# Masking the first batch's scores with one more TensorE product of constants per head

## Chip, cores and metric

One core of a Trainium2 chip runs the whole program. The metric is the device time of one execution in microseconds (us): the kernel before took 805.56 us, the median of three runs between 805.19 and 806.23.

## What is computed

Three stages on an input of 4 batches, 8 heads, 576 positions and 64 channels per head; the stages' results feed one another.

```python
scores = scale * np.matmul(q, k.transpose(0, 1, 3, 2))
mask = block_i >= block_j            # blocks of 64 positions
scores = np.where(mask, scores, -1000000000.0)
attn = softmax(scores); x = attn @ v # then heads side by side: (4, 576, 512)
k = np.maximum(xk @ w_k, 0.0); v = k * k @ w_v     # xk, xr: x mixed with its shifted self
x = sigmoid(xr @ w_r) * v
h = np.maximum(xt @ w_tok1, 0.0) @ w_tok2; u = x + h.T
out = u + np.maximum(u @ w_ch1, 0.0) @ w_ch2
```

The mask works in blocks of 64 positions. Where 128 rows of queries are taken at a time, the last 64 columns are masked for the upper 64 rows alone: a corner of 64 by 64.

## The kernel before

Attention goes by batch, by half of the queries (`hf` 0: positions 0 to 255, `hf` 1: the other 320) and by pair of heads (four pairs). Inside a half, `unit` (L515) works on 128 query rows, `j` = 0, 1 in the first half and 2, 3, 4 in the second; `j` = 4 has only 64 rows and takes both heads in one. A unit is a chain: `scores` (TensorE, into one of two PSUM tiles `s`), `mask` (VectorE memset of the corner to -8e9, L538, units j below 4 only), `largest` (VectorE maximum, L544), `bias` (L551 or L553), `exps` (ScalarE, L563), `sums` and `inverse` (L571 to L581), `first` (ScalarE, fp16 part of the probabilities, L587), `second` (VectorE, the rest in fp16, L593), `turn` (DMA transpose issued by SyncE, L599). `pv` (L602) multiplies the transposed probabilities by v (L646) and `total` brings them to SBUF as `xt` (L655, L657).

Behind attention, `channel_mix` (products at L751 and L756, into two PSUM tiles `l`) needs the four `xt` of a half: `mix` makes from them `mt` (L720, L726), `xh` (L732) and `xl` (L736). Then follow `front` (L914 to L966) and `back` (products at L764), which use TensorE almost alone.

Scores of batches 1 to 3 are made of three products of fp32r parts. Batch 0's are made of one product of plain fp32 operands (`load_qk` takes its short way for `b == 0`; `qk` at L504 then has one term). While batch 0's attention runs, the weights w_r, w_k and w_v are loaded and cut in high and low parts (`load_split`, `split_chunk`, L345 to L364), on ScalarE, VectorE and GpSimd.

The order on every engine is written out by a planner (`Plan.schedule`): each step has a cost, a due key, and reads and writes; for each engine the ready step with the smallest key is taken. Tables in `PLAN` (`lead_of`, `shift`, `lead_begin`) move the keys of a kind or a group of steps. Each engine then runs its list strictly in that order, waiting on semaphores.

```python
def mask():
    nc.vector.memset(s[:D, :, n - D:n], -8.0e9)
if j < 4:
    step("V", 0.14, ks, mask, r=[ts], w=[ts])
```

Of the kernel before, what the change touches and what calls it, by code (L numbers as in the profile page):

```python
# [8 lines left out]
F32 = mybir.dt.float32  # L9
# [41 lines left out]
        "attention.edge": -710.03, "back.<lambda>": 34.98, "back.g_group": -21.39, "back.g_high": -674.45,  # L51
        "back.g_low": -16.35, "back.rest": 162.8, "back.split": -271.85, "back.store": -779.77, "back.y_group":
        -49.32, "back.y_out": 128.07, "channel_mix.k_group": 0.52, "channel_mix.k_high": 122.36, "channel_mix.k_low":
        49.5, "channel_mix.k_out": 700.87, "channel_mix.r_group": -1.88, "channel_mix.r_out": 38.93,
        "channel_mix.square": -490.37, "channel_mix.store": 972.64, "channel_mix.v_group": -4.31, "channel_mix.v_out":
        138.59, "front.back_in": 734.14, "front.h1_high": -268.59, "front.h1_low": -80.29, "front.hidden": 281.6,
        "front.high": 274.43, "front.load": 776.08, "front.low": 678.84, "front.sum_u": 443.53, "front.turn": -120.46,
        "load_qk.high": 253.03, "load_qk.load": 185.56, "load_qk.low": 404.0, "load_qk.whole": 421.84,
        "load_v.gather": -15.3, "load_v.largest": -10.87, "load_v.load": 459.86, "load_v.one": 31.7, "load_v.power":
        182.97, "load_v.scale": 265.33, "load_v.spread": 478.19, "load_v.two": 729.5, "mix.here": -3.03, "mix.high":  # L60
        -14.49, "mix.low": 3.37, "mix.shifted": 147.07, "pv.products": -2.92, "pv.total": 92.69, "split_chunk.high":
        -63.89, "split_chunk.join": 6.76, "split_chunk.load": 143.85, "split_chunk.low": 282.21, "split_chunk.top":
        -112.45, "unit.bias": 105.96, "unit.exps": -239.76, "unit.first": -135.83, "unit.inverse": 471.77,
        "unit.largest": 1.71, "unit.mask": -0.69, "unit.scores": 481.59, "unit.second": 298.83, "unit.sums": 7.56,
        "unit.turn": -61.72,
# [15 lines left out]
        "attention.edge": 435.9, "back.<lambda>": 51.92, "back.g_group": -175.33, "back.g_high": -96.6, "back.g_low":  # L81
        174.47, "back.rest": 361.48, "back.split": 9.57, "back.store": -676.96, "back.y_group": -435.13, "back.y_out":
        -318.97, "channel_mix.k_group": -3.92, "channel_mix.k_high": 34.48, "channel_mix.k_low": 295.9,
        "channel_mix.k_out": 61.25, "channel_mix.r_group": -2.48, "channel_mix.r_out": 355.16, "channel_mix.square":
        181.93, "channel_mix.store": 254.58, "channel_mix.v_group": -1.74, "channel_mix.v_out": -95.22,
        "front.back_in": -799.64, "front.h1_high": -94.53, "front.h1_low": 327.36, "front.hidden": 242.72,
        "front.high": 556.49, "front.load": 51.98, "front.low": -83.46, "front.sum_u": 165.73, "front.turn": -324.84,
        "load_qk.high": -199.96, "load_qk.load": -251.86, "load_qk.low": 447.4, "load_qk.whole": 59.5,
        "load_v.gather": 96.8, "load_v.largest": -4.29, "load_v.load": 9.75, "load_v.one": 200.21, "load_v.power":
        74.15, "load_v.scale": -126.43, "load_v.spread": 91.47, "load_v.two": -460.37, "mix.here": 1.97, "mix.high":  # L90
        19.35, "mix.low": 63.96, "mix.shifted": 223.54, "pv.products": -1.86, "pv.total": 4.3, "split_chunk.high":
        191.37, "split_chunk.join": -2.04, "split_chunk.load": -58.89, "split_chunk.low": -104.87, "split_chunk.top":
        225.28, "unit.bias": 146.72, "unit.exps": 56.02, "unit.first": 220.91, "unit.inverse": -61.06, "unit.largest":
        0.1, "unit.mask": 86.57, "unit.scores": 187.42, "unit.second": -42.99, "unit.sums": -11.55, "unit.turn":
        -135.86,
# [14 lines left out]
def c_pe(n, k):  # L110
    return n / 2260 + 0.008 * k
# [194 lines left out]
class Kern:  # L306
# [71 lines left out]
    def attn_setup(self, pool):  # L378
        nc = self.nc
        self.eye = pool.tile([P, P], BF16, name="eye", bufs=1)  # L380
        self.ones = pool.tile([P, P], BF16, name="ones", bufs=1)
        self.step("G", 0.6, -1e3, make_identity, nc, self.eye, w=["eye"])
        self.step("V", 0.1, -1e3, nc.vector.memset, self.ones, 1.0, w=["ones"])
        self.pin = []
        for i in range(BUFS["pin"]):
            t = pool.tile([P, 2 * NJ * P], F16, name=f"pin{i}", bufs=1)
            self.step("V", 0.7, -1e3, nc.vector.memset, t, 0.0, w=[("pins", i)])
            self.pin.append(t)
# [115 lines left out]
    def qk(self, st, q0, parts):  # L504

        a, z = st["qk"][0], st["qk"][-1]
        terms = [a] if a is z else [a, (z[0], a[1]), (a[0], z[1])]
        for n, (q, k) in enumerate(terms):
            for o, e, k0, k1 in parts:
                self.nc.tensor.matmul(o, q[e, q0:q0 + P], k[e, k0:k1], start=n == 0, stop=n == len(terms) - 1)  # L510

    def unit(self, key, st, heads, j, begin):
# [857 lines left out]
```

## Time and profile before

| | us |
|---|---|
| median of three runs | 805.56 (805.19 to 806.23) |
| the profiled execution | 811.06 |
| its span, first to last instruction | 809.3 |
| TensorE busy in it | 763.7 (94%), granted clock 0.993 on average |
| VectorE busy | 477.3 (59%) |
| ScalarE busy | 419.2 (52%) |
| GpSimd busy | 181.3 (22%) |

The profile reports one execution. Its shares are means over stages of different kind, so it is read here by stretches: busy time of each engine in a stretch, the granted TensorE clock (1.00 is 2.4 GHz, 0.50 is 1.2 GHz), and the instructions in order of time with the idle time ahead of them in brackets. An instruction's duration on VectorE or ScalarE reaches a little into the next one's, so durations add up to somewhat more than the time taken.

### The profile page before, as it was taken

The page shows a single profiled execution, that of the slowest core. Times are in us where ns is not written, and L with a number is a line of the kernel's source. Part 1 is how long each engine was busy: PE and PEld are TensorE (multiplying, and loading weights), DVE is VectorE, ACT ScalarE, POOL GpSimd, SP SyncE. Part 2 cuts the span into 40 slices and gives each one's busy share as a digit, 9 for nine tenths or more (in the row PEclk, how much of TensorE's full clock was granted, in tenths as well). Part 3 has the DMA queues.
Part 4 walks back from the last instruction along what each step waited for, and adds up shares of the span by engine and source line. Part 5 has one row for each costly group of instructions (what it writes and reads, how often), then busy time and mean ns, then how long its engine had stood idle before and what let it go on. Part 6 is the DMA issues. An engine that isn't in the chain of part 4 may idle for free.

```text
span 809.3 us, 16129 instructions
## 1 busy us (share of the span) xinstructions
PE 763.7 (94%) x6120; PEld 661.7 (82%) x6120; DVE 477.3 (59%) x1194; ACT 419.2 (52%) x1070; POOL 181.3 (22%) x209
## 2 busy tenths in 40 slices
PE   2459999998999999999999999999999999999998
PEld 1227899887989999999999989998888888888886
DVE  7897898997798987789555687612212302301210
ACT  6887978687678795778564565502201201301100
POOL 3433524334145142432443222200000000000000
PEclk9999999999899999999999999999999999999999
DMA  8976964686465843566552654200000010000001
GB/s 272 269 189 106 201 148 115 146 170 120 113 138 125 159 117 93 117 140 113 191 180 84 232 170 141 78 27 1 14 26 1 14 39 14 1 26 14 14 13 40
DMA packets 136750, 84.30 MB, mean 104 GB/s; under 512 B 110944, under 2 KB 118240, under 8 KB 136160
## 3 DMA queue, kind: packets, MB, share of 16 engines
q1 hardware_dynamic: 136672, 83.27, 41.8%
q8 instruction: 48, 0.79, 0.4%
q14 instruction: 30, 0.25, 0.1%
HBM read 47.58 MB, written 9.44 MB: 70 GB/s over the span
## 4 chain that ended last, share of the span: by engine, by line
PE 81%; DVE 7%; DMA 5%; ACT 5%; issue 2%; SPq 0%; POOL 0%; ACTq 0%; DVEq 0%
PE b L764 37%; PE l L751 18%; PE l L756 9%; PE s L510 5%; PE o L646 4%; PE b L938 3%; PE b L959 3%; DMA pt<-pin 3%; DVE pin L593 2%; DMA wst<-in_w_k 1%; PE b L914 1%; DVE nm L544 1%; ACT pin L587 1%; ACT p L563 1%; DMA qkl<-in_w_v 1%
## 5 line engine op out<-in xcount | busy, mean ns | idle before, releaser
L1030 ACT ACTIVATE wy<-b 128x512 fp32r<-128x512 f32 (+1 forms) x60 | 33.3, 555 | 211.8 <-PE b L764 211.2
L764 PE MATMUL b<-uh,wx 128*128 128x512 f32 (+1 forms) x480 | 139.6, 373 | 0.0
L751 PE MATMUL l<-xh,wx 128*128 128x256 f32 (+1 forms) x768 | 123.7, 302 | 2.2 <-ACT r L792 1.8
L751 PEld LDWEIGHTS l<-xh,wx 128*128 128x128 f32 x768 | 107.9, 190 | 7.4 <-ACT r L792 2.0
L764 PE MATMUL b<-wy,c2a 128*128 128x512 f32 (+1 forms) x460 | 110.8, 367 | 0.0
L764 PEld LDWEIGHTS b<-uh,wx 128*128 128x128 f32 x480 | 87.2, 188 | 17.3 <-issue 0.2
L764 PEld LDWEIGHTS b<-wy,c2a 128*128 128x128 f32 x460 | 79.2, 189 | 15.3
L593 DVE SCALAR_TENSOR_TENSOR pin<-p,rs,pin 128x128 f16<-128x128 f32 (+4 forms) x112 | 77.0, 707 | 7.5 <-ACT pin L587 7.3
L1045 DVE TENSOR_TENSOR x<-b,x 128x256 f32<-128x256 f32 (+7 forms) x32 | 13.5, 454 | 114.8 <-PE b L764 114.8
L751 PE MATMUL l<-kh,wy 128*128 128x256 f32 (+1 forms) x512 | 78.1, 304 | 0.2 <-DVE ve L428 0.2
L646 PEld LDWEIGHTS <-vb 128*64 128x64 f16 x1920 | 52.9, 115 | 29.8 <-issue 13.7
L646 PE MATMUL o<-pt,vb 128*64 128x128 f16 (+1 forms) x1920 | 62.4, 220 | 14.3 <-DMA pt<-pin 7.2
L764 PE MATMUL b<-gx,wx 128*128 128x512 f32 x192 | 75.4, 393 | 0.0
L751 PEld LDWEIGHTS l<-kh,wy 128*128 128x128 f32 x512 | 71.5, 194 | 2.5 <-issue 1.4
L563 ACT ACTIVATE p<-s,nb 128x384 f32<-128x384 f32 (+4 forms) x112 | 61.6, 553 | 19.2 <-DVE nb L553 9.7
L587 ACT ACTIVATE pin<-p,rs 128x128 f16<-128x128 f32 (+4 forms) x112 | 63.2, 588 | 13.2 <-DMA pt<-pin 6.9
L756 PE MATMUL l<-xl,wx 128*128 128x320 f32 (+1 forms) x384 | 68.2, 300 | 0.0
L544 DVE TENSOR_REDUCE nm<-s 128x2 f32<-128x256 f32 (+4 forms) x80 | 63.6, 798 | 1.9 <-PE s L510 1.3
L756 PEld LDWEIGHTS l<-xl,wx 128*128 128x128 f32 x384 | 56.6, 190 | 2.1 <-issue 1.2
L1033 DVE SCALAR_TENSOR_TENSOR wy<-b,wy 128x512 fp32r<-128x512 f32 (+1 forms) x28 | 16.1, 576 | 62.8 <-ACT wy L1030 62.7
L1033 DVE SCALAR_TENSOR_TENSOR gx<-b,wy 128x512 fp32r<-128x512 f32 x32 | 21.9, 690 | 47.8 <-ACT wy L1030 47.8
L736 POOL TENSOR_TENSOR xl<-mt,xh 128x256 fp32r<-128x256 f32 (+1 forms) x32 | 28.4, 891 | 91.7 <-DVE xh L732 52.5
(116 smaller groups left out, 1397.0 us busy)
## 6 DMA issues: line engine op xcount, KB each, us to landing
wst<-in_w_c SPq DMA_DIRECT2D x24, 256.0 KB, 2.7
qkf<-in_kq SPq DMA_DIRECT2D x12, 480.0 KB, 3.5
v<-in_v SPq DMA_DIRECT2D x16, 320.0 KB, 3.1
x<-xd SPq DMA_DIRECT2D x4, 1152.0 KB, 7.0
wst<-in_w_c2a SPq DMA_DIRECT2D x18, 256.0 KB, 2.7
qkl<-in_w_v SPq DMA_DIRECT2D x16, 256.0 KB, 3.4
wst<-in_w_k SPq DMA_DIRECT2D x9, 410.0 KB, 5.4
qkf<-in_kq SPq DMA_DIRECT2D x12, 256.0 KB, 2.9
```

Source lines behind the costliest of these rows:

```text
L510: self.nc.tensor.matmul(o, q[e, q0:q0 + P], k[e, k0:k1], start=n == 0, stop=n == len(terms) - 1)
L544: nc.vector.tensor_reduce(out=c["nm"][:, :nh], in_=m, axis=AX.XY if j == 4 else AX.X, op=ALU.max, negate=True)
L563: nc.scalar.activation(out=c[x], in_=s, func=AF.Exp, scale=0.125, bias=c["nb"][:, x:x + 1], accum_out=c["sm"][:, x:x + 1],)
L587: nc.scalar.activation(out=like(pin[:, :n]), in_=c[x], func=AF.Copy, scale=rs)
L593: nc.vector.scalar_tensor_tensor(out=like(pin[:, w:w + n]), in0=c[x], scalar=rs, in1=like(pin[:, :n]), op0=ALU.mult, op1=ALU.subtract)
L646: nc.tensor.matmul(o[hh * D:hh * D + D, q0:q0 + rows], v[:, i, y, hh, :], st["pt", hh, j][:, x * (j + 1) + i, :], start=i == x == y == 0, ...
L736: (nc.vector if i in pl["xl_d"] else nc.gpsimd).tensor_tensor(out=l, in0=x[i], in1=raw(x["h"][i]), op=ALU.subtract)
L751: self.nc.tensor.matmul(ps, ww[:, k, :], x[0][k], start=k == 0 and n == 0, stop=False)
L756: self.nc.tensor.matmul(ps, w[0][:, k, :], x[1][k], start=False, stop=k == kt - 1)
L764: self.nc.tensor.matmul(ps, ww[k], xx[k], start=k == 0 and n == 0, stop=k == kt - 1 and n == 2)
L1030: nc.scalar.activation(out=gh(m), in_=d["g", m][:, :n], func=AF.Relu)
L1033: nc.vector.scalar_tensor_tensor(out=gl(m), in0=d["g", m][:, :n], scalar=0.0, in1=raw(gh(m)), op0=ALU.max, op1=ALU.subtract)
```

## The change

For batch 0 the VectorE memset of the corner is dropped. After a unit's score product, each head gets one more product accumulated on the last 64 columns: `mq` (its first 64 columns 1, its last 64 columns 0) by `mk` (all -2^27), over 64 rows, which adds -2^33 to the upper 64 query rows of the corner and 0 to the lower ones. Both constants are written by three memsets at the start. Units of batches 1 to 3, and j = 4, are as before. The planner's cost of the score step is not raised. The tables `lead_of`, `shift` and `lead_begin` have new numbers throughout.

```diff
     lead_of={
-        "attention.edge": -710.03, "back.<lambda>": 34.98, "back.g_group": -21.39, "back.g_high": -674.45,
+        "attention.edge": -741.87, "back.<lambda>": 250.25, "back.g_group": -80.15, "back.g_high": -948.97,
...
+        self.mq = pool.tile([P, P], F32, name="mq", bufs=1)
+        self.mk = pool.tile([P, D], F32, name="mk", bufs=1)
+        self.step("V", 0.1, -1e3, nc.vector.memset, self.mq[:, :D], 1.0, w=[("mq", 0)])
+        self.step("V", 0.1, -1e3, nc.vector.memset, self.mq[:, D:], 0.0, w=[("mq", 1)])
+        self.step("V", 0.1, -1e3, nc.vector.memset, self.mk, -2.0**27, w=[("mq", 2)])
...
-    def qk(self, st, q0, parts):
+    def qk(self, st, q0, parts, masked=False):
...
-                self.nc.tensor.matmul(o, q[e, q0:q0 + P], k[e, k0:k1], start=n == 0, stop=n == len(terms) - 1)
+                self.nc.tensor.matmul(
+                    o, q[e, q0:q0 + P], k[e, k0:k1], start=n == 0, stop=n == len(terms) - 1 and not masked
+                )
+        for o, e, k0, k1 in parts if masked else ():
+            self.nc.tensor.matmul(o[:, k1 - D:], self.mq[e], self.mk[e], start=False, stop=True)
...
-                self.qk(st, q0, [(s[:, y, :n], half[y], 0, n) for y in range(2)])
+                self.qk(st, q0, [(s[:, y, :n], half[y], 0, n) for y in range(2)], masked)
...
+        masked = not split and j < 4
-        step("PE", cost if split else c_pe(4 * n, 2) if j < 4 else c_pe(4 * n, 4), key, scores, r=st["tqk"], w=[ts], mode="half" if j < 4 else "")
+        step("PE", cost if split else c_pe(4 * n, 2) if j < 4 else c_pe(4 * n, 4), key, scores, r=list(st["tqk"]) + ["mq"] * masked, w=[ts],
+             mode="half" if j < 4 else "")
-        if j < 4:
+        if j < 4 and not masked:
             step("V", 0.14, ks, mask, r=[ts], w=[ts])
```

Lines behind L381 move by 6, behind `qk` by 10 to 12: the score product is L516 in the changed kernel, the new product L520, the maximum L554, `second` L603, the products with v L658, channel mix L763 and L768.

The start of VectorE's list, from the end of the constants on. Before, the corner's memset (L538) stands ahead of each maximum:

```order
9 L679 MEMSET xt_129 128x1
10 L679 MEMSET xt_131 128x1
11 L679 MEMSET xt_133 128x1
12 L679 MEMSET xt_135 128x1
13 L538 MEMSET s 64x2x64
14 L404 TENSOR_REDUCE vm<-v_101 128x1
15 L544 TENSOR_REDUCE nm<-s 128x2
16 L412 TENSOR_SCALAR vm<-vm 128x1
17 L538 MEMSET s 64x2x64
18 L553 TENSOR_SCALAR nb<-nm 128x2
19 L544 TENSOR_REDUCE nm<-s 128x2
```

The same place in the changed kernel:

```order
11 L691 MEMSET xt_136 128x1
12 L691 MEMSET xt_138 128x1
13 L691 MEMSET xt_140 128x1
14 L691 MEMSET xt_142 128x1
15 L554 TENSOR_REDUCE nm<-s 128x2
16 L410 TENSOR_REDUCE vm<-v_103 128x1
17 L563 TENSOR_SCALAR nb<-nm 128x2
18 L554 TENSOR_REDUCE nm<-s 128x2
19 L418 TENSOR_SCALAR vm<-vm 128x1
```

The memsets are gone; the maximum of v (`vm`) now stands behind the first maximum of scores and ahead of its bias `nb`.

TensorE's list where the first product of the channel mix stands (L751, `l<-xh,wx`), before:

```order
403 L646 LDWEIGHTS vb
404 L646 MATMUL o<-pt_711,vb 64x64
405 L646 LDWEIGHTS vb
406 L646 MATMUL o<-pt_711,vb 64x64
407 L751 MATMUL l<-xh,wx 128x256 x8
408 L756 MATMUL l<-xl,wx 128x256 x4
409 L751 MATMUL l<-xh,wx 128x256 x8
410 L756 MATMUL l<-xl,wx 128x256 x4
411 L751 MATMUL l<-xh,wx 128x256 x8
412 L756 MATMUL l<-xl,wx 128x256 x4
```

The same place in the changed kernel (L763):

```order
467 L658 LDWEIGHTS vb
468 L658 MATMUL o<-pt_845,vb 64x128
469 L658 LDWEIGHTS vb
470 L658 MATMUL o<-pt_872,vb 64x128
471 L428 LDWEIGHTS ones
472 L428 MATMUL l<-vd,ones 128x128
473 L763 MATMUL l<-xh,wx 128x256 x8
474 L768 MATMUL l<-xl,wx 128x256 x4
475 L763 MATMUL l<-xh,wx 128x256 x4
476 L658 LDWEIGHTS vb
477 L658 MATMUL o<-pt_891,vb 64x128
478 L658 LDWEIGHTS vb
```

Ahead of the channel mix there now stand 16 score units where 14 stood (one more with j = 3 and one more with j = 4), 216 products with v where 192 stood, and five where there were four of the small products with `ones`; and the channel mix's groups have products with v between them (32, then 40) where they followed one another. Of the 16 masked units, 14 stand ahead of the channel mix.

VectorE's list up to the last `xh` that the first channel-mix product reads (L732 before, its last row here):

```order
144 L538 MEMSET s 64x2x64
145 L732 CAST xh<-mt 128x256
146 L726 SCALAR_TENSOR_TENSOR mt<-xt_133,mu,mt 128x256
147 L726 SCALAR_TENSOR_TENSOR mt<-xt_131,mu,mt 128x256
148 L593 SCALAR_TENSOR_TENSOR pin_93<-p,rs,pin_93 128x384
149 L593 SCALAR_TENSOR_TENSOR pin_90<-p,rs,pin_90 128x384
150 L736 TENSOR_TENSOR xl<-mt,xh 128x256
151 L538 MEMSET s 64x2x64
152 L732 CAST xh<-mt 128x256
```

In the changed kernel (L744), with the row behind it:

```order
148 L603 SCALAR_TENSOR_TENSOR pin_92<-s,rs,pin_92 128x512
149 L669 TENSOR_SCALAR xt_142<-o,vo 128x256
150 L585 TENSOR_SCALAR rs<-sm 128x1
151 L410 TENSOR_REDUCE vm<-v_773 128x1
152 L591 RECIPROCAL rs<-rs 128x1
153 L738 SCALAR_TENSOR_TENSOR mt<-xt_142,mu,mt 128x256
154 L738 SCALAR_TENSOR_TENSOR mt<-xt_138,mu,mt 128x256
155 L418 TENSOR_SCALAR vm<-vm 128x1
156 L738 SCALAR_TENSOR_TENSOR mt<-xt_136,mu,mt 128x256
157 L744 CAST xh<-mt 128x256
158 L603 SCALAR_TENSOR_TENSOR pin_93<-p,rs,pin_93 128x576
```

Up to that `xh`, VectorE's list has lost 13 corner memsets and won: 3 memsets of the constants, 2 joins of w_v pieces (`qkl`, 256 columns), one maximum of v, one maximum over 576 and one over 1024 columns, 2 `second` of 512 columns from PSUM, one `mt` of 256 columns, and 7 short ones (one on `vm`, two each of `nb`, `rs` and its inverse); one `xl` and one short copy of `xt` have gone behind it. ScalarE's list up to the last `xh` that it makes for that product has won ten instructions: one cast and two high parts of w_v, one exp of 576 and two of 512 columns, one `first` of 576 and two of 512, and one `total` of 320 columns.

## Rows read from the trace of the kernel before

**Rows 1.** Busy time by stretch: us, PE, PEld, DVE, ACT, POOL, PEclk, DMA share, GB/s
```profile
0.00:65.00 65.00, 30.86 (x252) 16.68 (x252) 56.44 (x157) 49.99 (x134) 26.49 (x35) 1.00 0.89 242
65.00:165.00 100.00, 97.78 (x1032) 86.89 (x1026) 85.47 (x226) 80.68 (x219) 39.38 (x44) 0.98 0.68 143
```
**Rows 2.** Timeline of PE: start us, us, line, tiles, form, count [idle before]
```profile
18.48 0.80 PE L510 MATMUL s<-qk 64*128 64x128 f32 x4 [0.36 <-ACT p L563]
39.61 2.08 PE L510 MATMUL s<-qk 64*128 64x512 f32 x4
61.80 3.31 PE L646 MATMUL o<-pt,vb 128*64 128x128 f16 x96
65.04 1.21 PE L751 MATMUL l<-xh,wx 128*128 128x256 f32 x8
66.56 1.11 PE L751 MATMUL l<-xh,wx 128*128 128x256 f32 x8
69.90 1.56 PE L751 MATMUL l<-xh,wx 128*128 128x256 f32 x8 [1.76 <-ACT r L792]
92.25 1.13 PE L510 MATMUL s<-qk 64*128 64x512 f32 x4
95.57 1.24 PE L510 MATMUL s<-qk 128*128 128x288 f32 x4
```
**Rows 3.** Timeline of DVE: around one corner memset, and the last xh
```profile
28.48 0.17 DVE L538 MEMSET s<- 64x128 f32 x1
28.56 0.35 DVE L544 TENSOR_REDUCE nm<-s 128x2 f32<-128x256 f32 x1
...
63.93 0.27 DVE L732 CAST xh<-mt 128x256 fp32r<-128x256 f32 x1
```
**Rows 4.** DVE groups of one form: count | busy us, mean ns of one | idle before
```profile
L538 DVE MEMSET s<- 64x128 f32 x64 | 10.5, 165 | 7.5 <-PE s L510 5.9
L355 DVE SCALAR_TENSOR_TENSOR qkl<-qkl,tw 128x256 uint32<-128x256 uint32 x16 | 8.1, 505 | 2.7 <-ACT tw L352 2.7
L404 DVE TENSOR_REDUCE vm<-v 128x1 f32<-128x640 f32 x16 | 12.8, 800 | 0.0
L544 DVE TENSOR_REDUCE nm<-s 128x1 f32<-128x576 f32 x16 | 11.9, 744 | 1.3 <-PE s L510 1.3
L544 DVE TENSOR_REDUCE nm<-s 128x2 f32<-128x1024 f32 x16 | 19.4, 1211 | 0.1
L593 DVE SCALAR_TENSOR_TENSOR pin<-s,rs,pin 128x512 f16<-128x512 f32 x8 | 6.0, 748 | 3.1 <-ACT pin L587 3.1
L726 DVE SCALAR_TENSOR_TENSOR mt<-xt,mu,mt 128x256 f32<-128x256 f32 x32 | 17.1, 550 | 0.5 <-ACT mt L720 0.4
L736 DVE TENSOR_TENSOR xl<-mt,xh 128x256 fp32r<-128x256 f32 x16 | 8.0, 498 | 1.4 <-ACT xh L732 1.4
```
**Rows 5.** ACT groups of one form, same columns
```profile
L563 ACT ACTIVATE p<-s,nb 128x576 f32<-128x576 f32 x16 | 11.8, 737 | 3.2 <-DVE pin L593 2.4 <-DVE nb L553 0.7
L563 ACT ACTIVATE s<-s,nb 128x512 f32<-128x512 f32 x8 | 5.3, 665 | 0.7 <-DVE nb L553 0.3 <-DVE rs L575 0.2
L587 ACT ACTIVATE pin<-p,rs 128x576 f16<-128x576 f32 x16 | 12.3, 769 | 3.3 <-issue 2.5 <-DMA pt<-pin 0.8
L587 ACT ACTIVATE pin<-s,rs 128x512 f16<-128x512 f32 x8 | 5.4, 689 | 1.3 <-DMA pt<-pin 0.8 <-DVE pin L593 0.5
```
**Rows 6.** Busy time in two stretches where PE stood still, columns as in rows 1
```profile
68.00:74.00 6.00, 4.24 (x22) 3.90 (x20) 4.66 (x12) 6.00 (x19) 2.23 (x3) 0.72 0.48 128
196.00:208.00 12.00, 8.95 (x97) 8.34 (x96) 6.22 (x18) 6.64 (x22) 4.88 (x5) 0.72 0.90 161
```
**Rows 7.** Timeline of ACT: the cast that stands ahead of the first r (L792)
```profile
68.00 0.48 ACT L352 CAST tw<-qkl 128x256 f16<-128x256 bf16 x1 [3.62 <-DMA qkl<-in_w_v]
```
**Rows 8.** Tile pt from 55 to 80 us: transposes from issue to landing
```profile
DMA to landing us min/median/max: 3.3/3.9/5.4
```
**Rows 9.** PE's waits from 165 to 260 us: total us, times, longest us
```profile
PE o L646 <- DMA pt<-pin: 3.4, 3, 2.8
```

More of the change, by code (lines that the diff above doesn't have):

```diff
@@ L50 @@
     lead_of={
-        "attention.edge": -710.03, "back.<lambda>": 34.98, "back.g_group": -21.39, "back.g_high": -674.45,
[L52 to L65, printed above, removed]
+        "attention.edge": -741.87, "back.<lambda>": 250.25, "back.g_group": -80.15, "back.g_high": -948.97,
@@ new lines @@
+        "back.g_low": 560.14, "back.rest": -111.54, "back.split": -275.94, "back.store": -511.84, "back.y_group":
+        -379.47, "back.y_out": -241.06, "channel_mix.k_group": 0.97, "channel_mix.k_high": 251.86,
+        "channel_mix.k_low": 318.37, "channel_mix.k_out": 681.33, "channel_mix.r_group": -1.77, "channel_mix.r_out":
+        -98.93, "channel_mix.square": -573.06, "channel_mix.store": 1011.38, "channel_mix.v_group": 1.21,
+        "channel_mix.v_out": 363.38, "front.back_in": 708.49, "front.h1_high": -54.85, "front.h1_low": 8.28,
@@ new lines @@
+        "front.hidden": 348.84, "front.high": -72.12, "front.load": 973.86, "front.low": 146.72, "front.sum_u": -1.18,
+        "front.turn": -419.87, "load_qk.high": 117.98, "load_qk.load": 120.27, "load_qk.low": 580.3, "load_qk.whole":
+        543.69, "load_v.gather": 17.14, "load_v.largest": -24.55, "load_v.load": 591.48, "load_v.one": 13.28,
+        "load_v.power": 36.16, "load_v.scale": 210.24, "load_v.spread": 654.69, "load_v.two": 1200.65, "mix.here":
+        -3.86, "mix.high": -6.4, "mix.low": -8.87, "mix.shifted": 506.1, "pv.products": 383.09, "pv.total": 88.52,
@@ L66 @@
+        "split_chunk.high": 38.47, "split_chunk.join": -77.56, "split_chunk.load": 129.03, "split_chunk.low": 322.59,
+        "split_chunk.top": -118.74, "unit.bias": 197.86, "unit.exps": -292.57, "unit.first": -185.58, "unit.inverse":
+        479.75, "unit.largest": 13.06, "unit.mask": -360.42, "unit.scores": 805.18, "unit.second": 495.55,
+        "unit.sums": 57.34, "unit.turn": 28.05,
     },
     shift={
[8 rows of a table removed]
[8 rows of a table added]
     },
@@ L80 @@
     lead_begin={
[L81 to L95, printed above, removed]
+        "attention.edge": 361.23, "back.<lambda>": -313.95, "back.g_group": -179.81, "back.g_high": -201.61,
@@ new lines @@
+        "back.g_low": 327.6, "back.rest": 516.79, "back.split": -133.8, "back.store": -916.64, "back.y_group":
+        -250.61, "back.y_out": -190.79, "channel_mix.k_group": -2.87, "channel_mix.k_high": -113.95,
+        "channel_mix.k_low": 147.7, "channel_mix.k_out": 200.98, "channel_mix.r_group": 8.56, "channel_mix.r_out":
+        680.83, "channel_mix.square": 282.06, "channel_mix.store": -51.61, "channel_mix.v_group": -2.31,
+        "channel_mix.v_out": 133.71, "front.back_in": -920.81, "front.h1_high": -284.96, "front.h1_low": 406.89,
@@ new lines @@
+        "front.hidden": -127.43, "front.high": 486.5, "front.load": -67.24, "front.low": -4.23, "front.sum_u": 292.69,
+        "front.turn": -149.83, "load_qk.high": -112.87, "load_qk.load": -134.31, "load_qk.low": 483.45,
+        "load_qk.whole": 30.01, "load_v.gather": 26.44, "load_v.largest": -7.99, "load_v.load": -38.05, "load_v.one":
+        284.67, "load_v.power": 150.61, "load_v.scale": -142.77, "load_v.spread": 186.73, "load_v.two": -366.11,
+        "mix.here": 41.29, "mix.high": 34.53, "mix.low": 44.96, "mix.shifted": 429.43, "pv.products": 5.57,
@@ L96 @@
+        "pv.total": -107.06, "split_chunk.high": 194.41, "split_chunk.join": 37.21, "split_chunk.load": -49.25,
+        "split_chunk.low": 30.99, "split_chunk.top": 238.86, "unit.bias": 264.15, "unit.exps": 218.25, "unit.first":
+        270.66, "unit.inverse": 177.82, "unit.largest": -4.68, "unit.mask": 333.41, "unit.scores": 286.88,
+        "unit.second": 165.07, "unit.sums": -0.75, "unit.turn": -205.66,
     },
```

16 rows, old and new, of the table shift are left out of this document.

## The prediction

> **What bounds the kernel now.** I read the busy time by stretch first, because the shares of the whole span mix two kinds of stage. Up to 65 us TensorE works for 30.86 us and VectorE for 56.44, ScalarE for 49.99; in the next 100 us TensorE works for 97.78 [rows 1]. So there is a front of some 65 us that VectorE sets, with ScalarE close behind, in which TensorE stands idle for 34 us, and then a long part that TensorE sets. The end is the front's length, plus TensorE's work that is left behind it, plus what TensorE stands still there.
>
> The timeline of TensorE gives the border: the first product of the channel mix begins at 65.04, behind 96 products with v that began at 61.80 [rows 2]. The last `xh` that it reads was made at 63.93 + 0.27 = 64.20 [rows 3], so VectorE had 0.84 us to spare there.
>
> Behind the border the reader should look for stretches in which TensorE is neither busy nor at full clock. There are two large ones. From 68 to 74 us it is busy for 4.24 of 6 us at a mean granted clock of 0.72: 1.76 us idle, and about 6 x 0.28 = 1.7 us lost to the clock. From 196 to 208 us it is busy for 8.95 of 12, also at 0.72: 3.05 us idle, about 12 x 0.28 x 8.95/12 = 2.5 lost to the clock [rows 6]. The first comes from one wait: the third group of the channel mix, at 69.90, waits 1.76 us for `r` to empty its PSUM tile [rows 2], and that `r` stands on ScalarE behind a cast of w_v which waited 3.62 us for its load [rows 7]. Most of the second is a product with v that waits for a DMA transpose: three such waits from 165 to 260 us, 3.4 us together, the longest 2.8 [rows 9].
>
> **The change part by part.** The sum is made against the profiled execution, which took 811.06 us with a span of 809.3 (1.76 us lie around it). It lies 5.5 us above the median of 805.56, so I work with differences and carry them to the median.
>
> *Memsets.* Of the 16 that go, 13 stood in VectorE's list ahead of the border. One is written as 165 ns [rows 4], but the maximum behind it starts 0.08 us after the memset does [rows 3]. So they give between 13 x 0.08 = 1.0 and 13 x 0.165 = 2.1 us. As I count all VectorE work by such mean durations, I take 2.1. The three behind the border give nothing, since TensorE sets the time there. The three memsets of constants stand at VectorE's very start, a short one each: 3 x 0.165 = 0.5 at most, which I leave with the short ones below.
>
> *Work moved ahead of the border on VectorE.* By the lists and [rows 4]: two `qkl` joins 2 x 0.505, one maximum of v 0.800, one maximum over 576 columns 0.744, one over 1024 columns 1.211, two `second` 2 x 0.748, one `mt` 0.550; less one `xl` 0.498. That is 5.3. The short ones (three memsets and seven others, less one that left) are nine at up to about 0.11, some 1.0. Together +6.3, and with the memsets **+4.2**. VectorE is busy for 56.44 of the front's 65 us, so part of this can fall where it waits now: between 0 (8.6 us of idle would hold all) and 4.2. I take the busy share, 4.2 x 56.44/65 = 3.6, and subtract the 0.84 us that it had to spare: **front +2.8**. ScalarE gets one exp of 576 columns, two of 512, one `first` of 576 and two of 512: 0.737 + 2 x 0.665 + 0.769 + 2 x 0.689 = 4.2 [rows 5], and some smaller ones, but it has 15 us of idle in the front against VectorE's 8.6; I let VectorE decide. The upper end for the front is 5.
>
> *TensorE's work that this takes from behind the border.* One more unit with j = 3 (1.13), one with j = 4 (1.24), and 24 products with v, 24 x 3.31/96 = 0.83 [rows 2]. These now lie in TensorE's 34 us of idle: **-3.2**.
>
> *The mask products.* Score units of the first batch take 0.80 us for 128 columns and 2.08 for 512 in the front [rows 2]. The slope is 1.28/384 us per column, so 64 more columns on both heads are 0.21; if they cost like a unit of their own, the line through both rows gives 0.59 at 64 columns. 14 of the 16 pairs lie in TensorE's idle of the front and cost only as a link of the chain (a rival below). Two lie behind the border, where the same form takes 1.13 instead of 2.08 [rows 2], nearly the ratio of the clock's two levels (though the clock's column reads 1.00 in the front, [rows 1]): 2 x 0.54 x 0.21 = 0.2 to 0.6. They follow on products of the same form without a wait, so I take the slope: **+0.2**.
>
> *The stall behind the border.* Before, three groups of the channel mix followed one another, and the third needed a `r`. Now 32 products with v stand inside the second group and 40 between the second and the third: 72 x 3.31/96 = 2.5 us of work ahead of the wait that was 1.76 long [rows 2]. So that wait goes, though two w_v casts still stand on ScalarE between the last `xh` and the first `r`. What is late next are the 40: they read a transpose whose `second` VectorE makes directly behind the last `xh`, in about 0.8 us (512 columns take 0.748 [rows 4]). Transposes at this place landed 3.9 us after issue, between 3.3 and 5.4 [rows 8]: 4.7 us after the border. TensorE comes to them after two groups of 1.52 (65.04 to 66.56) and the 32: 3.04 + 1.10 = 4.1 us [rows 2]. A wait of 0.6 is left (0 to 2.1) where 1.76 was: **-1.2**. Of the 1.7 us lost to the clock there I give back half, the clock having fallen at that very standstill: **-0.8**; the bounds are 0 and -1.7.
>
> Sum: 2.8 - 3.2 + 0.2 - 1.2 - 0.8 = -2.2, so **803.4 us**. With the bounds (front 0 to 5, mask 0.2 to 0.6, stall -3.5 to 0) my own case reaches from about 800.5 to 807. About 0.2%, 1.6 us, is what a measurement of this kernel can tell from no change.
>
> **The rivals.** *More stalls go (faster).* All tables are new, and in the list the products with v stand in other places relative to their transposes. If the standstill of 196 to 208 us goes as well, 3.05 + 2.5 = 5.5 us come on top: 797.9, and 800.6 for half of it. For: these are short waits on a few late transposes, which another order can cover. Against: nothing in the lists aims at that place.
>
> *A new wait for a transpose (slower).* The same freedom can open one. The front now has VectorE and ScalarE carry work of later units earlier, products with v stand between channel-mix groups, and each reads a transpose that lands 3.3 to 5.4 us after its issue. One more standstill like that of 196 to 208 costs 5.5 us and the time becomes 808.9. It decides from about 2.2 + 1.6 = 3.8 us of added waiting with the clock's loss; below that the sign stays mine or becomes no change. For: the 40 products already stand 0.6 us too early by my count, and up to 2.1.
>
> *The mask product lengthens the chain (slower).* In the front a unit is scores, mask, maximum, bias, exp, and two PSUM tiles alternate. The memset cost 0.08 to 0.165 us in that chain, the two products 0.21 to 0.59. If all 14 units feel it, the front grows by 14 x (0.21 - 0.165) = 0.6 to 14 x (0.59 - 0.08) = 7.1 us: 804.0 to 810.5, the middle 807. Against: VectorE has other work in its list between units, and waits for `s` only part of the time. The Trainium skill bears on the price (page "FP8 and Floating Point Precision", section "TensorE Precision Notes"): true fp32 takes four passes through the array. By that, an estimate, a 64-column product at the slower of the two speeds, 1.2 GHz, takes 4 x 64/1200 = 0.21 us, two heads one after the other 0.43, and 14 units 6.0 us in the chain where the slope of the rows gives 0.21 and 3.0 for both heads; the sum would be 803.4 + 14 x (0.43 - 0.165) = 807.1. No row here separates the heads.
>
> *The change does nothing.* If work that leaves one place of the front comes back at another, the front just shifts with what it took along, +2.8 - 3.2, and the stall stays: 805.4. This is the lower half of my own case and gets no chance of its own.
>
> **How the numbers follow.** My forecast 0.48, of which 0.30 is faster by over 0.2%, 0.12 within it and 0.06 slower. More stalls go 0.18, all faster. A new wait 0.20, of which 0.17 slower and 0.03 within. The longer chain 0.14: 0.02 faster, 0.06 within, 0.06 slower. Faster 0.50, same 0.21, slower 0.29. Below 798.5 lies the rival's full price (0.08), above 810 two new waits or the dearest chain (0.10): the range is 798.5 to 810. My own case alone reaches from 800.5 to 807.
>
> **What would show it.** Each step right: the first channel-mix product at about 67.8 us; 48 corner memsets; 32 mask products, 28 of them in the first 68 us; under 1 us of idle on TensorE in the 10 us behind that product, and no wait for `r` there. Wrong: a border later than 70 us (then ScalarE or the chain set it), VectorE's idle for `s` grown from unit to unit (then the mask product is in the chain), or new lines "products with v wait for the transpose" of over 3.4 us in a stretch where there were none.

## The result, and the profile after

The changed kernel is slower: 817.70 us median of four runs (815.51 to 819.63) against 805.89 us (805.19 to 806.39), a ratio of 1.0146 with a 95% interval of 1.0116 to 1.0177. The prediction said 803.4 us, the range 798.5 to 810.0. Size and sign are wrong. The execution profiled first took 819.63 us, the slowest of the four, with a span of 817.9. Each ratio below is to runs of the kernel before that were made together with that kernel's.

The border, the first product of the channel mix, is where to look first. Busy time of the changed kernel ahead of it and behind it (columns as in [rows 1]):

```profile
0.00:74.94 74.94, 39.03 (x342) 27.55 (x342) 61.34 (x161) 57.02 (x150) 29.51 (x38) 0.91 0.97 234
74.94:817.90 742.96, 731.55 (x5846) 641.26 (x5844) 419.25 (x1020) 363.79 (x920) 152.08 (x171) 1.00 0.38 90
```

The front lasts 74.94 us where it lasted 65.04 [rows 2], 9.9 us more against the 2.8 forecast. VectorE is busy for 61.34 us in it and idle for 13.6, where it was 56.44 and 8.6 of 65 [rows 1]. So its work grew by 4.9, where 4.2 were added up; its waits, which the prediction let shrink, grew by 5. Their list for VectorE ahead of the border (total us, times, longest):

```profile
DVE wst L355 <- ACT wst L352: 5.3, 6, 2.5
DVE pin L603 <- ACT pin L597: 1.7, 4, 0.8
DVE nm L554 <- PE s L520: 1.6, 3, 0.7
```

The largest item, 5.3 of the 13.6 us, are waits for a weight piece that ScalarE casts; for the maximum behind the new product VectorE waits 1.6 us in all. The timeline of TensorE (answers to [rows 2]) shows the new product, a new standstill, and the border:

```profile
23.67 0.53 PE L520 MATMUL s<-mk,mq 64*128 64x64 f32 x4
24.13 1.07 PE L658 MATMUL o<-pt,vb 128*64 128x128 f16 x16
...
60.61 1.77 PE L658 MATMUL o<-pt,vb 128*64 128x64 f16 x56 [3.54 <-DMA pt<-pin]
...
74.94 1.19 PE L763 MATMUL l<-xh,wx 128*128 128x256 f32 x8
75.96 0.64 PE L768 MATMUL l<-xl,wx 128*128 128x256 f32 x4
76.44 0.63 PE L763 MATMUL l<-xh,wx 128*128 128x256 f32 x4
77.00 0.24 PE L658 MATMUL o<-pt,vb 128*64 128x128 f16 x1
77.64 1.05 PE L658 MATMUL o<-pt,vb 128*64 128x128 f16 x31 [0.39 <-DMA pt<-pin]
78.62 0.75 PE L763 MATMUL l<-xh,wx 128*128 128x256 f32 x4
...
82.41 0.33 PE L520 MATMUL s<-mk,mq 64*128 64x64 f32 x4
82.67 0.75 PE L768 MATMUL l<-xl,wx 128*128 128x256 f32 x4
```

A pair of mask products takes 0.46 us from start to start here in the front and 0.26 behind the border, inside the bounds given. At 60.61 TensorE has waited 3.54 us for a transpose, inside the front. In the first 20 us behind the border no wait for `r` is left; the 32 products with v wait 0.39 us for their transposes, and the 40 that follow do not wait.

### The profile page after: what moved, and what is told of

Read it like the earlier page. It is cut to its first block, busy times and chain, and to the rows that moved or that the text cites. A ratio compares the mean times of both kernels' runs of the same rounds, so it can differ in the third digit from the quotient of the medians.

```text
span 817.9 us, 16260 instructions
## 1 busy us (share of the span) xinstructions
PE 770.6 (94%) x6184; PEld 668.8 (82%) x6184; DVE 480.6 (59%) x1181; ACT 420.8 (51%) x1070; POOL 181.6 (22%) x209
## 4 chain that ended last, share of the span: by engine, by line
PE 53%; DMA 1%; ACT 0%; DVE 0%; issue 0%; SPq 0%; ACTq 0%
PE b L776 37%; PE l L763 6%; PE b L950 3%; PE b L971 3%; PE l L768 3%; PE b L926 1%; DMA x<-xd 1%; PE o L658 1%; DMA pt<-pin 0%; PE s L516 0%; ACT pin L597 0%; DVE bxl L937 0%; DVE x L1057 0%; ACT p L573 0%; ACT bxh L930 0%
## 5 line engine op out<-in xcount | busy, mean ns | idle before, releaser
L763 PE MATMUL l<-xh,wx 128*128 128x256 f32 (+1 forms) x768 | 124.7, 300 | 2.0 <-DVE ve L434 2.0
L763 PEld LDWEIGHTS l<-xh,wx 128*128 128x128 f32 x768 | 108.0, 188 | 6.2 <-DVE ve L434 2.6
L776 PEld LDWEIGHTS b<-wy,c2a 128*128 128x128 f32 x460 | 79.1, 189 | 15.2
L763 PE MATMUL l<-kh,wy 128*128 128x256 f32 (+1 forms) x512 | 76.9, 300 | 0.8 <-ACT kt L832 0.4
L603 DVE SCALAR_TENSOR_TENSOR pin<-p,rs,pin 128x128 f16<-128x128 f32 (+4 forms) x112 | 71.2, 656 | 9.0 <-ACT pin L597 8.3
L658 PE MATMUL o<-pt,vb 128*64 128x128 f16 (+1 forms) x1920 | 64.5, 221 | 10.5 <-DMA pt<-pin 7.8
L573 ACT ACTIVATE p<-s,nb 128x128 f32<-128x128 f32 (+4 forms) x112 | 61.9, 555 | 22.7 <-DVE nb L563 14.5
L763 PEld LDWEIGHTS l<-kh,wy 128*128 128x128 f32 x512 | 70.0, 189 | 3.4 <-issue 1.0
L658 PEld LDWEIGHTS <-vb 128*64 128x64 f16 x1920 | 53.2, 116 | 22.7 <-issue 15.5
L768 PE MATMUL l<-xl,wx 128*128 128x320 f32 (+1 forms) x384 | 68.3, 300 | 0.0
L554 DVE TENSOR_REDUCE nm<-s 128x2 f32<-128x512 f32 (+4 forms) x80 | 63.7, 802 | 5.0 <-PE s L520 2.8
L768 PEld LDWEIGHTS l<-xl,wx 128*128 128x128 f32 x384 | 55.9, 188 | 2.1 <-issue 0.9
L516 PE MATMUL s<-qk 64*128 64x128 f32 (+4 forms) x80 | 26.6, 680 | 27.1 <-ACT p L573 18.7
L748 POOL TENSOR_TENSOR xl<-mt,xh 128x256 fp32r<-128x256 f32 (+1 forms) x32 | 31.6, 990 | 74.7 <-DVE xh L744 61.4
```

Source lines behind the costliest of these rows:

```text
L554: nc.vector.tensor_reduce(out=c["nm"][:, :nh], in_=m, axis=AX.XY if j == 4 else AX.X, op=ALU.max, negate=True)
L573: nc.scalar.activation(out=c[x], in_=s, func=AF.Exp, scale=0.125, bias=c["nb"][:, x:x + 1], accum_out=c["sm"][:, x:x + 1],)
L603: nc.vector.scalar_tensor_tensor(out=like(pin[:, w:w + n]), in0=c[x], scalar=rs, in1=like(pin[:, :n]), op0=ALU.mult, op1=ALU.subtract)
L658: nc.tensor.matmul(o[hh * D:hh * D + D, q0:q0 + rows], v[:, i, y, hh, :], st["pt", hh, j][:, x * (j + 1) + i, :], start=i == x == y == 0, ...
L748: (nc.vector if i in pl["xl_d"] else nc.gpsimd).tensor_tensor(out=l, in0=x[i], in1=raw(x["h"][i]), op=ALU.subtract)
L763: self.nc.tensor.matmul(ps, ww[:, k, :], x[0][k], start=k == 0 and n == 0, stop=False)
```

## The experiments

**Product or order?** Four kernels keep the planner's order of one kernel step for step and change the mask alone. *First:* the order of before, with the products.

```diff
         def mask():
             s = c["s"]
-            nc.vector.memset(s[:D, :, n - D:n], -8.0e9)
+            if split:
+                nc.vector.memset(s[:D, :, n - D:n], -8.0e9)
...
-                self.qk(st, q0, [(s[:, y, :n], half[y], 0, n) for y in range(2)])
+                self.qk(st, q0, [(s[:, y, :n], half[y], 0, n) for y in range(2)], not split)
```

> The planner's order of the kernel before, kept step for step; in the first batch the corner's memset is replaced by the mask products. Theory A (the new order makes the front longer): within 1.5 us of before, 804.5 to 807.5, first channel-mix product at 64 to 66.5 us. Theory B (the product lengthens the chain scores, mask, maximum in each of 14 units, 0.47 us instead of 0.08 to 0.17): 14 x 0.3 to 14 x 0.39 = 4 to 5.5 us more, 810 to 812, first channel-mix product at 69 to 71 us.

Measured: 807.98 us, ratio 1.0013 (0.9994 to 1.0032). The border stands at 65.94 us. The time is 1.4 us above the kernel before's beside it (806.58), as theory A said, though 0.5 above the range in figures.

*Second:* the order of the changed kernel, with memsets; the products' loop in `qk` is dropped.

```diff
         def largest():
...
+            if masked:
+                nc.vector.memset(s[:D, :, n - D:n], -8.0e9)
```

> The planner's order of the changed kernel, kept step for step; the mask products are left out and the memset stands right ahead of each maximum, as before. Theory A: 814 to 819 us, as the changed kernel. Theory B: 4 to 5.5 us below the changed kernel or more, 806 to 813.

Measured: 817.88 us, 1.0126 (1.0083 to 1.0168). *Third and fourth:* the same two orders with neither (the two diffs without their product or memset).

> The planner's order of the changed kernel with neither products nor memsets in the first batch (its 16 masked units are left unmasked, so the first batch's attention is computed without the corner's mask). Theory A: 812 to 818 us, at most 2 below the memset in the same order. Theory B: as with the memset in the same order or lower, 805 to 812.

> The planner's order of the kernel before with the first batch's 16 memsets left out and nothing in their place (the first batch's attention is computed without the corner's mask). It bounds what the memsets can be worth: 13 x 0.08 to 13 x 0.165 us, 803.5 to 805; both theories say the same, and if it is 805.9 the memsets stood beside other work.

Measured: 814.82 us in the new order, 1.0098 (1.0062 to 1.0133), and 805.67 in the old, 0.9988 (0.9964 to 1.0013). Theory A holds: with either mask the new order gives 817.7 to 817.9 (ratios 1.0146 and 1.0126), and the product in the old order changes nothing that can be told from no change. Two figures were missed: without a mask the new order is 3.1 us below the memset in the same order, where at most 2 was said, and the old order is above 803.5 to 805. Removing the memsets alone gave 0.9 us, which cannot be told from nothing. Busy time ahead of each kernel's border, in the order in which the runs are told here:

```profile
0.00:65.94 65.94, 35.12 (x305) 24.26 (x305) 55.74 (x148) 49.80 (x134) 26.07 (x35) 1.00 0.89 240
```
```profile
0.00:72.78 72.78, 33.59 (x285) 19.05 (x286) 64.24 (x172) 56.07 (x148) 28.83 (x38) 0.91 0.93 237
```
```profile
0.00:70.19 70.19, 34.24 (x285) 19.73 (x286) 61.23 (x161) 56.37 (x149) 29.75 (x38) 0.90 0.96 247
```
```profile
0.00:64.70 64.70, 30.78 (x252) 16.57 (x252) 55.15 (x144) 49.93 (x135) 26.12 (x35) 1.00 0.89 244
```

VectorE is busy for 55 to 56 us ahead of the border in the old order and for 61 to 64 in the new one, whatever the mask. In the old order the product moves the border by 1.2 us against no mask (64.70 to 65.94).

**Numbers or rules?** The changed kernel with the three tables of before, so that the planner meets 16 steps fewer with the old numbers:

```diff
-        "attention.edge": -741.87, "back.<lambda>": 250.25, "back.g_group": -80.15, "back.g_high": -948.97,
+        "attention.edge": -710.03, "back.<lambda>": 34.98, "back.g_group": -21.39, "back.g_high": -674.45,
...
```

> The changed kernel with the three tables of numbers of the kernel before: the planner sees that 16 steps are gone from VectorE and orders anew by the old numbers. TensorE's list then has some 60 more rows ahead of the first channel-mix product than before. Theory W: border by the added work, 67 to 71 us, 808 to 813 us. Theory R, or no cost of moved work: 65 to 67 us, 806 to 809 us.

Measured: 823.13 us, 1.0207 (1.0176 to 1.0237), the border at 75.54; both expectations are missed. The old numbers with 16 steps less give an order worse than either; the new numbers win some 5 of its 17 us back.

**Which part of the order?** Three kernels put one order's front and the other's rest, or one's choice and the other's arrangement, together. The steps are run by a written list, and a step whose buffer is still in use is put behind the next one that has its own; the buffers `pin` and `tw` are dealt out anew along the list.

```diff
-        order = self.schedule()
-        for s in order:
+        self.schedule()
+        queue, steps, out = [self.steps[i] for i in ORDER], [], set()
...
+        for s in steps:
...
             s.fn(*s.args)
```

> Mask products as in the changed kernel. Ahead of the first channel-mix product stand exactly the steps that stood there in the kernel before, but arranged in the changed kernel's relative order; behind it the order of the kernel before. Theory W (the border is late because more work was moved ahead of it: the three units, the products with v and two weight pieces that are new there): first channel-mix product at 65.5 to 68 us, 806 to 810 us. Theory R (the relative order inside the front makes the engines wait on each other and on loads, whatever the amount): 70 to 73 us, 811 to 815 us.

> The opposite: ahead of the first channel-mix product stand the steps that stand there in the changed kernel, arranged in the relative order of the kernel before; behind it the order of the changed kernel. Theory W: 71 to 74 us for the first channel-mix product, 813 to 817 us. Theory R: 66 to 69 us, 807 to 811 us.

> The changed kernel's order up to the first channel-mix product, and from there the order of the kernel before (the 17 steps that the changed kernel left out of the front stand behind the first two groups). It tells what the rest of the new order costs. If the rest costs nothing: the same border as the changed kernel, 74 to 75.5, and 816 to 819 us. If the finer mixing of products behind the border costs time (24 more changes of kind in TensorE's list, at some 0.1 us, and more waits): 812.5 to 815.5 us.

Measured: 834.15, 837.80 and 841.10 us (ratios 1.0327, 1.0392 and 1.0428), with the border at 92.4, 85.3 and 72.5 us. All miss both expectations. In the first, VectorE waits for TensorE's scores and TensorE for ScalarE's `p`, as if units that had overlapped now followed one another (a reading that was not tested); two of the longest waits from 30 to 92 us:

```profile
DVE nm L777 <- PE s L743: 15.1, 4, 6.2
PE s L739 <- ACT p L796: 13.5, 4, 4.9
```

So these three don't tell W from R, and no other run does. What they do show is that parts of two orders cannot be added up: each was worse than both wholes.

**Do the DMA engines set the front?** That is theory D, which the prediction had not weighed. What they moved in the first 65 us before and 75 us after:

```profile
DMA packets 17181, 15.74 MB, mean 242 GB/s; under 512 B 12568, under 2 KB 12568, under 8 KB 17176
```
```profile
DMA packets 20629, 17.52 MB, mean 234 GB/s; under 512 B 15630, under 2 KB 15630, under 8 KB 20622
```

It is 1.78 MB more, and the DMA engines are busy for 0.97 of the time instead of 0.89 [rows 1]. Two kernels in the old order with products load more: seven extra loads of 256 KB, and a control of 2 KB each.

```diff
             nc.sync.dma_start(h[:, 1:4 * k + 1], src)
+            if tok[0] == "wk" and 1 <= tok[1] <= 7:
+                nc.sync.dma_start(self.spare_load[tok[1] - 1][:, :1024], src[:, :1024])
```

> Mask products in the order of the kernel before, as in the first experiment, and beside seven of the loads of w_k one more load each, 256 KB of w_k into a DRAM scratch that nobody reads: 1.8 MB more in the front, and no work for the computing engines. Theory D (the front's length is set by the DMA engines, which are 88 to 97% busy in it at about 240 MB per ms): the first channel-mix product comes 5 to 7.5 us later than the 65.9 us of the first experiment, 71 to 74 us, and the time is 812 to 816 us. Theory W (VectorE's work sets it): 65.5 to 67.5 us, 807 to 809.5 us.

> The control: the same seven additional loads, of 2 KB each instead of 256 KB. What it costs is SyncE's time of issue. Both theories: 65.5 to 67.5 us for the first channel-mix product, 807 to 809.5 us.

Measured: 812.27 us (1.0063, 1.0037 to 1.0090) with the border at 69.7, and 808.79 (1.0031, 1.0013 to 1.0050) with the border at 67.8. With more bytes the time is inside theory D's range and the border short of it; the control's border is late as well, by 0.3 us. Two kernels load less, half of each piece of w_k:

```diff
-            nc.sync.dma_start(h[:, 1:4 * k + 1], src)
+            m = 4 * k if tok[0] != "wk" else 2 * k
+            nc.sync.dma_start(h[:, 1:m + 1], src[:, :m])
```

> The changed kernel, but each of the ten loads of w_k brings only the first half of its columns (the rest of the tile keeps what was there, so w_k is wrong in half of its values): 2.05 MB less in the front, the same instructions on every engine. Theory D: the first channel-mix product comes 5 to 8.5 us earlier than in the changed kernel, at 66 to 70 us, 808 to 813 us. Theory W: 73 to 75.5 us, 815 to 819 us.

> The same halving of the loads of w_k (half of w_k's values are wrong) in the order of the kernel before with mask products. Theory D: the first channel-mix product at 59 to 63 us, 800 to 804 us. Theory W: 65 to 66.5 us, 806 to 809 us.

Measured: 816.11 us in the new order (1.0112, 1.0085 to 1.0139), the border at 70.9; 806.70 in the old (0.9995, 0.9978 to 1.0013), at 66.0. Theory D falls as the account of the loss: 2.05 MB less bring nothing in the old order, and in the new one the time is theory W's and the border lies between both ranges; the gain there, 1.6 us by the medians, is not clear of noise (1.0112 against 1.0146, with overlapping intervals). More bytes can cost: 1.8 MB more took 3.5 us over the control, though these two intervals overlap a little, and 1.9 us at the border. VectorE's work stays the same there; its idle time is 13.4 us against 11.0 (more bytes, control, fewer bytes in the new order):

```profile
0.00:69.70 69.70, 33.34 (x305) 23.32 (x305) 56.33 (x148) 50.42 (x135) 26.23 (x35) 1.00 0.96 254
```
```profile
0.00:67.80 67.80, 35.66 (x305) 24.84 (x305) 56.80 (x149) 50.24 (x135) 26.08 (x35) 1.00 0.90 235
```
```profile
0.00:70.90 70.90, 37.73 (x342) 26.78 (x342) 62.36 (x161) 55.87 (x149) 29.96 (x38) 0.93 0.88 215
```

**A second look at both kernels**, unchanged, so that one execution's accidents can be told from the kernel:

> The kernel before, unchanged, in a second execution under the profile. If the stalls belong to the kernel: TensorE busy 4.0 to 4.6 of 6 us from 68 to 74 us and some 9 of 12 from 196 to 208, both at a granted clock near 0.7, and a time near 811 us. If they belong to the one execution profiled: 5.7 us or more of 6 and 11 or more of 12, the clock 1.00, and a time of 804 to 807 us.

> The changed kernel, unchanged, in a second execution under the profile. If the waits for weight pieces belong to the order: first channel-mix product at 74 to 75.5 us, VectorE idle for about 13 us ahead of it. If they are the execution's: 71 to 73.5 us, VectorE idle for 8.5 to 11 us, and 815 to 818 us. VectorE's busy time ahead of the border stays at 61 to 62.5 us in both.

Measured: 804.15 us and 816.97 us. Busy time of the kernel before: ahead of the border, behind it, and in the two stretches of [rows 6]:

```profile
0.00:64.60 64.60, 30.61 (x253) 16.09 (x253) 56.11 (x157) 49.94 (x134) 26.51 (x35) 1.00 0.87 244
64.60:802.40 737.80, 728.96 (x5871) 641.18 (x5868) 423.04 (x1038) 368.59 (x936) 155.17 (x175) 1.00 0.40 93
...
68.00:74.00 6.00, 6.00 (x45) 5.00 (x44) 5.28 (x16) 5.86 (x18) 4.38 (x5) 1.00 0.26 80
196.00:208.00 12.00, 11.21 (x151) 10.20 (x145) 10.46 (x31) 9.15 (x27) 2.81 (x4) 1.00 0.66 165
```

Both stalls are gone: they belonged to the one execution that the prediction was argued from, 811.06 us against a median of 805.56. The five other profiled kernels in the old order have a mean granted clock of 0.999 or 1.000; that execution had 0.993. The changed kernel the second time, and three stretches up to its border:

```profile
0.00:71.80 71.80, 38.07 (x342) 26.57 (x342) 61.86 (x161) 56.63 (x150) 29.34 (x38) 0.90 0.98 243
71.80:815.20 743.40, 731.68 (x5846) 641.24 (x5844) 418.07 (x1021) 364.67 (x921) 152.20 (x171) 1.00 0.38 90
...
56.00:60.00 4.00, 1.77 (x54) 1.77 (x55) 2.33 (x4) 1.79 (x6) 1.25 (x1) 0.64 1.21 119
60.00:65.00 5.00, 4.26 (x35) 2.64 (x31) 4.53 (x15) 4.54 (x12) 2.04 (x2) 0.50 0.78 217
65.00:71.80 6.80, 5.04 (x46) 3.04 (x42) 6.29 (x16) 5.71 (x14) 2.36 (x3) 0.57 1.05 239
```

About 3 us of the front's waits were the first execution's (the border stands at 71.80, VectorE's idle time is 9.9). Between the two second executions lie 12.8 us of span. Of these, 7.2 lie in the front, which on VectorE are 5.75 of work (56.11 to 61.86) and 1.45 of waits; 5.6 lie behind the border, 2.7 of them TensorE's busy time (728.96 to 731.68) and 2.9 its idle time.

This account does not show that VectorE set the front. ScalarE's work there grew by 6.7 us and TensorE's by 7.5, and their idle times, 14.7 and 34.0 us, are 15.2 and 33.7. What came last at the border stands in the second execution's timeline:

```profile
58.23 2.13 PE L658 MATMUL o<-pt,vb 128*64 128x64 f16 x56 [3.79 <-DMA pt<-pin]
...
66.98 1.65 PE L516 MATMUL s<-qk 64*128 64x384 f32 x4 [1.76 <-ACT p L573]
...
68.74 2.02 PE L516 MATMUL s<-qk 64*128 64x512 f32 x4
70.55 0.46 PE L520 MATMUL s<-mk,mq 64*128 64x64 f32 x4
70.94 0.86 PE L658 MATMUL o<-pt,vb 128*64 128x128 f16 x24
...
71.78 1.19 PE L763 MATMUL l<-xh,wx 128*128 128x256 f32 x8
```
```profile
69.69 0.69 ACT L744 CAST xh<-mt 128x256 fp32r<-128x256 f32 x2
```

The last `xh` was ready at 70.38, 1.4 us ahead of the border (63.71 and 0.9 in the kernel before's second execution). TensorE came to the border later, for it had waited 1.76 us for ScalarE's `p` and then worked without a pause from 66.98. In that stretch stands a unit with j = 3, which takes 2.2 us with its mask: there are three such units ahead of the border where there were two. So `xh` is some 7 us late, and TensorE's own list, behind ScalarE's, is later still.

The longest standstill, at 58.23, is in both executions of the changed kernel. There TensorE waited 3.79 us and ScalarE 2.19 us for a transpose which landed 7.1 us after its issue; in the kernel before the longest from 45 to 75 us took 5.4 and 4.7. Fewer bytes of w_k left it at 7.2. With the memset, or without a mask, the longest in the same order took 6.0 and 5.6, so the order alone does not settle it, and why it is late stays open.

**The two pieces of w_v** that the new order brings ahead of the border, put behind it by the same kind of list:

> The changed kernel with one thing moved: the eight steps (two loads, one cast of the upper part, one join, two high and two low parts) of w_v that stand ahead of the first channel-mix product in the new order and behind it in the old one are put right behind that product. If moved work costs what it takes on the engines: 0.4 us less on VectorE and 1.3 less on ScalarE, and 0.5 MB less to load, so 0.5 to 2 us, 815.5 to 817.5 us, border at 71 to 74 us. If these pieces are the main cause: 808 to 812 us. If they are covered: no change from the changed kernel.

Measured: 823.15 us, 1.0199 (1.0162 to 1.0236), 5.5 us more than the changed kernel, with the border at 71.5: all three expected times are missed. Ahead of the border these pieces cost no more than 0.3 us; the time behind it grew from 743.4 to 749.1 us, which reads as if they came too late there. None of these kernels is faster than the kernel before beyond doubt.

## Why the prediction was wrong, step by step

Between the two second executions the three parts of the sum came out as follows. The front was forecast at +2.8 us and came to +7.2. TensorE's work behind the border was forecast at -3.2 + 0.2 and came to +2.7. Its stalls there were forecast at -1.2 - 0.8 and came to +2.9. The misses, 4.4, 5.7 and 4.9 us, are the 15.0 between -2.2 and +12.8. The bounds that the prediction names also add up to 799.1 to 808.0 us, and not to its 800.5 to 807.

**VectorE's moved work** was priced somewhat low: +4.2 forecast with the memsets taken off, +4.9 in the first executions and +5.75 in the second. What failed is the step after it, "I take the busy share ... and subtract the 0.84 us that it had to spare". Idle time did not take the work up, on VectorE or on ScalarE, which the prediction left out for its 15 us of idle; with the same mask (memset, product or none) VectorE's busy time ahead of the border is 5.6 to 8.1 us longer in the new order than in the old, and its idle time is between 8.5 and 10.2 us in both, but for the 13.6 of the changed kernel's first execution. The front came out 7.2 us longer, not 2.8, and the bound named for it, 5, was too narrow. The prediction's own sign against this step came true: a border later than 70 us, with ScalarE's `p` and TensorE's chain of units last. That putting the moved work back would win the front back was not shown, since the three kernels made of parts tell nothing on it; which dependence inside the new order adds the waits is not settled.

**The work taken from behind the border** (-3.2): the step "These now lie in TensorE's 34 us of idle" failed twice. The score units did leave the place behind the border, but in the front TensorE's idle time stayed at 34 us and a unit with j = 3 stands in the stretch without a pause that ends at the border. And TensorE's busy time behind the border rose by 2.7 us. The products of the kernel before behind the border, second execution, by line (count | busy us, mean ns):

```profile
L751 PE MATMUL l<-xh,wx 128*128 128x256 f32 (+1 forms) x768 | 122.5, 300 | 0.5 <-ACT kt L820 0.5
L751 PE MATMUL l<-kh,wy 128*128 128x256 f32 (+1 forms) x512 | 76.7, 300 | 0.2 <-DVE ve L428 0.2
L756 PE MATMUL l<-xl,wx 128*128 128x320 f32 (+1 forms) x384 | 67.8, 299 | 0.0
L646 PE MATMUL o<-pt,vb 128*64 128x128 f16 (+1 forms) x1731 | 50.6, 212 | 1.3 <-DMA pt<-pin 0.9 <-DVE vb L446 0.3
L756 PE MATMUL l<-kl,wy 128*128 128x256 f32 (+1 forms) x256 | 39.9, 299 | 0.0
L510 PE MATMUL s<-qk 128*128 128x288 f32 (+2 forms) x24 | 6.9, 519 | 0.1
```

and of the changed kernel:

```profile
L763 PE MATMUL l<-xh,wx 128*128 128x256 f32 (+1 forms) x768 | 124.9, 301 | 2.0 <-DVE ve L434 2.0
L763 PE MATMUL l<-kh,wy 128*128 128x256 f32 (+1 forms) x512 | 76.9, 299 | 0.8 <-ACT kt L832 0.4 <-DVE nb L563 0.2 <-DVE r L893 0.2
L768 PE MATMUL l<-xl,wx 128*128 128x320 f32 (+1 forms) x384 | 68.3, 300 | 0.0
L658 PE MATMUL o<-pt,vb 128*64 128x128 f16 (+1 forms) x1706 | 51.7, 212 | 2.7 <-DMA pt<-pin 2.6
L768 PE MATMUL l<-kl,wy 128*128 128x256 f32 (+1 forms) x256 | 40.4, 300 | 0.0
L516 PE MATMUL s<-qk 128*128 128x288 f32 (+2 forms) x16 | 4.5, 510 | 0.1
```

The score products of the first batch fell by 2.4 us (24 records to 16). But the same 1920 products of the channel mix, at the same mean duration of one, fill 310.5 us where they filled 306.9, and fewer products with v fill 1.1 us more. In TensorE's list kinds of products change 220 times from the border to the last channel-mix product, 196 times before. A group cut in two shows what that costs, in the first timeline behind the result, from start to start: eight products from 74.94 to 75.96, 1.02 us; four and four with products with v between them 0.56 (76.44 to 77.00) and 0.58 (78.62 to 79.20), 1.14.

The same can be counted over the whole stretch in both second executions, from each product's start to the next one's start. Inside a run of channel-mix products a step takes 120 ns at 256 columns and 147 at 320 in both kernels. The first step of a run takes 217 to 232 ns, and the last, ahead of another kind of product, 202 to 221. There are 90 runs where there were 78, and what their first and last steps take above an inner step makes 2.6 of the 3.2 us by which the channel mix grew in this count. So the finer mixing is most of that excess; why the products with v fill more stays open. The prediction moved products as if each carried only its own time.

**The stall behind the border** (-1.2 and -0.8) was not the kernel's to give back: that term is 0, and so is the rival that counted on the second stall. The prediction had said that its execution lay 5.5 us above the median and had not asked where those 5.5 us were. It foresaw rightly that the wait for `r` close behind the border goes. The 0.6 us that it left were ahead of the 40 products, which do not wait; the 32 ahead of them wait, 0.39 us and in the second execution 0.91, so that the size is near is luck.

**The mask product**: +0.2 behind the border was forecast; two pairs at 0.26 from start to start are 0.5, inside the bounds of 0.2 to 0.6. The estimate from the Trainium skill (page "FP8 and Floating Point Precision", section "TensorE Precision Notes": four passes for true fp32) was 0.43 for a pair at the slower of the two speeds; the trace has 0.46 for the slow pairs of the front, and agrees. As a link in the chain it costs little: of the rival's 0.6 to 7.1 us the old order shows 0.9 to 1.3 at the border (65.94 against 65.04 and 64.6) and, by its interval, at most 0.32% in time.

**The new wait for a transpose** was a rival with the right sign, and too small: behind the border TensorE waits 2.6 us for transposes instead of 0.9, and for `ve` 2.0 instead of 0.2. The largest new one, 3.5 us, stands in the front, where the prediction had not looked. A front that grows by more than the work moved into it, and a TensorE that is busier behind the border with less to do there, are none of the rivals.

Not weighed at all were the loads, 1.78 MB more up to the border. The runs with more and with fewer bytes put them at a few us at most, not at 10.

## What to carry to other kernels

When an edit re-deals a planner's order, price the new order as an order. Do not count on idle time to take up work that is moved ahead into a stage: here VectorE, ScalarE and TensorE kept about the idle time that they had, and the stage grew by about as much as their work. Look for what ends last at the stage's border, on every engine that it reads from. On the engine that sets the rest, each further change of kind has a price too. The edit itself is best measured with the old order held fixed; here its cost could not be told from nothing, and the order cost 1.1 to 1.3%. Before a gain is counted from a stall, look whether the profiled execution lies above the median, for the stall may be what put it there.

## What was not expected of the hardware

In the front, score products take about 1.8 times what they take later, while the granted clock is printed as 1.00 for its first 40 us. The same form of the changed kernel at four times:

```profile
17.91 1.65 PE L516 MATMUL s<-qk 64*128 64x384 f32 x4 [1.18 <-ACT p L573]
...
54.22 0.96 PE L516 MATMUL s<-qk 64*128 64x384 f32 x4
...
69.45 1.65 PE L516 MATMUL s<-qk 64*128 64x384 f32 x4 [2.00 <-ACT p L573]
...
81.66 0.92 PE L516 MATMUL s<-qk 64*128 64x384 f32 x4
```

The trace holds no record of the clock ahead of 54.3 us, where the first one says full clock, and the column reads 1.00 where it has none. From 69.4 to 71.1 us it reads 0.50, and the form takes the same 1.65 us as at 17.91; at 54.22 it takes 0.96. So a printed 1.00 at the start of a profile does not say that products ran at 2.4 GHz; by these durations they ran at 1.2.

In the changed kernel's second execution the printed clock falls to between 0.50 and 0.64 from 56 to 71.8 us, behind a standstill of TensorE for a transpose, and TensorE carries out the last units of the front at that clock. Against the kernel before this is no new loss: its score products of 512 columns take 2.08 us in the front [rows 2], and this one's 2.02 at 68.74. And in a front whose DMA engines are printed as 89% busy, 2 MB less to load bring nothing in the old order, so that figure alone does not name the bound.
